# Two attention + FFN layers on one core: VectorE exponentials as four shifted bit patterns summed by PE, one weight ring, LayerNorm transposes by DMA

## The chip, the cores and the metric

The kernel runs on one core of one Trainium2 chip. The metric is device time in microseconds (us) of one execution; where a number is a median, its runs are named. PE is the matrix engine (PEld its weight loads), ACT is ScalarE, DVE is VectorE, POOL is GpSimd, SP issues the DMAs. SBUF and PSUM are the two on-chip memories in which the tiles lie; PE writes its results into PSUM (tile `ps` in the lines below). "The profile" is a page on one execution; "the trace" is what that page is made from. A line number such as L875 is a line of the kernel that the profile is of; an inserted line shifts the numbers below it.

## The reference

Two layers, each an attention block and an FFN, with LayerNorm in front of each and a residual around each:

```python
def _A_ref(x, wqkv, wo):                     # B=1, S=2048, D=512, H=32 heads of 16
    qkv = (x @ wqkv).reshape(B, S, 3, H, 16) ...
    scores = einsum("bhqd,bhkd->bhqk", q, k) * 16 ** -0.5
    p = softmax(scores, axis=-1)
    o = einsum("bhqk,bhkd->bhqd", p, v)
    return o.reshape(B, S, D) @ wo
def _B_ref(x, w1, b1, w2, b2):               # F=1792
    return gelu_tanh(x @ w1 + b1) @ w2 + b2
x = x + _A_ref(layernorm(x)); x = x + _B_ref(layernorm(x))   # twice
```

The scores are the large part: 2 layers x 32 heads x 2048 x 2048. The kernel cuts them into 4096 "cells" of 128 keys x 512 queries of one head.

## The kernel before

A small scheduler in Python builds the instruction order of every engine before the launch. Each piece of work is a generator that yields operations with a guessed cost; the scheduler picks the ready one of the highest priority. On the chip the order is then fixed: an engine whose next instruction waits does nothing else meanwhile.

Per cell, PE makes the scores in a PSUM bank (2 KB a partition), ACT or DVE exponentiates them into SBUF, and PE multiplies the result with V. A V block has 17 columns, the last of them ones, so that the same matmul gives the sum of the exponentials. A pass that takes results out of PSUM, and so frees the bank, is called an eviction here. ACT takes cells in groups of three and two banks; some cells go to DVE, through one of two spare banks (6 and 7), which the projections, the FFN and the transposes need too.

```python
SLOTS = ((0, 1, 2), (3, 4))                       # banks of ACT's two groups
    # exps(): ACT, 2 or 3 cells at a time
    yield _Op("act", ..., lambda e, ...: e.activation(out=dst, in_=src, func=ACT.Exp, scale=0.25), ...)
    # dfirst(): DVE takes a cell out of PSUM as a bf16 bit pattern of 2**x with a linear mantissa
    yield _Op("dve", DV, lambda e: e.tensor_scalar(T["DU"][:, du, j, :], self.bank(b), E_SCALE, E_BIAS,
              op0=ALU.mult, op1=ALU.add), ...)
    # dchain(): three cells at a time, six passes that correct the mantissa
    ... tensor_scalar(m, u, 127, None, op0=ALU.bitwise_and)
    ... tensor_scalar(x, m, -128.0, None, op0=ALU.add)
    ... tensor_tensor(out=x, in0=x, in1=m, op=ALU.mult)
    ... tensor_scalar(v, m, E_B, E_A, op0=ALU.mult, op1=ALU.add)
    ... tensor_tensor(out=v, in0=x, in1=v, op=ALU.mult)
    ... tensor_tensor(out=u, in0=u, in1=v, op=ALU.add)
```

The FFN runs in the background of the attention. Its GELU takes three passes on POOL, a tanh on ACT and one pass on DVE, for 49 pairs of 128-row blocks (the last query chunk uses ACT's own GELU):

```python
    # hpair(): x2 and g2 are 128 x 1024
    yield _Op("pool", 2.2, lambda e: e.tensor_tensor(out=x2, in0=g2, in1=g2, op=ALU.mult), ...)
    yield _Op("pool", 0.8, lambda e: e.tensor_scalar(x2, x2, 8.0 * C2, 2.0 * C1, op0=ALU.mult, op1=ALU.add), ...)
    yield _Op("pool", 2.2, lambda e: e.tensor_tensor(out=x2, in0=x2, in1=g2, op=ALU.mult), ...)
    yield _Op("act", 1.05, lambda e: e.activation(out=x2, in_=x2, func=ACT.Tanh), ...)
    yield _Op("dve", 1.15, lambda e: e.scalar_tensor_tensor(out=g2, in0=x2, scalar=1.0, in1=g2, op0=ALU.add, op1=ALU.mult), ...)
```

The softmax here doesn't subtract the row's maximum and nothing guards it: scores larger than these inputs give would overflow.

Of the kernel before, what the change touches and what calls it, by code (L numbers as in the profile page):

```python
# [12 lines left out]
D = 512  # L13
H = 32
# [5 lines left out]
SLOTS = ((0, 1, 2), (3, 4))  # L20
CELLS = 3
PT_RING = 5
QP_RING = 3
W1_RING = 3

DB = 3
DU = 3
DMIN = 24
LOG2E = 1.4426950408889634
E_SCALE = 0.25 * LOG2E * 128  # L30
E_BIAS = 127.0 * 128
E_A = 0.0023795
E_B = 0.00061147 / 128
# [133 lines left out]
class _Sched:  # L167
# [17 lines left out]

    def spawn(self, gen, prio):
        self.threads.append(_Thread(gen, prio, self.nseq))
        self.nseq += 1

    def _advance(self, th):  # L190
        moved = False
        while th.op is None and not th.done:
# [25 lines left out]
            if isinstance(item, _Op):  # L218
                th.op = item
                if item.prio is None:  # L220
                    item.prio = th.prio
            elif item[0] in ("acq", "need", "take", "cond"):
                th.block = item
            elif item[0] == "rel":
                self.pools[item[1]].append(item[2])
            elif item[0] == "give":
                self.tokens[item[1]] = item[2] if len(item) > 2 else True
            elif item[0] == "spawn":
                self.spawn(item[1], item[2])
# [63 lines left out]
def bass_interleave_layers__mha_block__dense_activation_gelu__prompt_kernel(  # L293
# [15 lines left out]
    with ExitStack() as es:  # L309
        def sb(shape, dt, name):  # L310
# [4 lines left out]
        T["WQKV"] = sb([128, 3, NDC, D], BF16, "wqkv")  # L315
        T["WO"] = sb([128, NDC, D], BF16, "wo")
        T["W1"] = sb([128, W1_RING, NDC, 256], BF16, "w1")
# [8 lines left out]
        T["XN"] = sb([128, NDC, 512], BF16, "xn")  # L326
        T["XLN"] = sb([128, 3, D], BF16, "xln")
        T["G"] = sb([128, NFC, 512], BF16, "g")
        T["X2"] = sb([128, 2, 1024], BF16, "x2")
        T["PT"] = sb([128, PT_RING, CELLS, 512], BF16, "pt")  # L330
        T["PART"] = [v[:, 0:8192].bitcast(F32).rearrange("p (g q) -> p g q", g=8) for v in vf[::-1]]
        T["DU"] = sb([128, DU, DB, 512], U16, "du")
        T["DM"] = sb([128, DB * 512], U16, "dm")
        T["DW"] = sb([128, DB * 512], F16, "dw")
# [17 lines left out]
        sem_names = ["pe", "act", "dve", "pool", "dx0", "dx1", "dx2", "dx3", "dwq", "dwk", "dwv", "dwo", "db1", "db2",  # L352
                     "dw10", "dw11", "dw12", "dw2", "dout"]
# [28 lines left out]
MM = 0.22  # L382
SW = 0.11
ST = 0.36
# [4 lines left out]
class _Plan:  # L389
# [8 lines left out]
    def init(self):  # L398
# [11 lines left out]
        yield _Op("dve", 0.6, lambda e: e.memset(self.bank(5), 0.0), writes=["B.5"])  # L410
# [9 lines left out]
    def loads(self):  # L420
# [22 lines left out]
        yield load(T["WO"][:], hbm["wo"].rearrange("(c p) f -> p c f", p=128), "dwo", ["WO"], 2.5)  # L443
# [32 lines left out]
    def ln_tile(self, c, t, dst, dkeys):  # L476
# [4 lines left out]
            reads=["X.%d" % t, "RSTD.%d" % c, "NMR.%d" % c], writes=["XLN.%d" % x])  # L481
        b = yield ("acq", "misc")
# [10 lines left out]
    def proj(self, l, kind, i, c, src, skeys, ph, done):  # L493

        T = self.T
        for t in ([i] if kind == "V" else range(4 * c, 4 * c + 4)):
            yield ("need", ("lnt", t, ph))
        b = yield ("acq", "misc")
        pb = self.bank(b)
        W = T["WQKV"]  # L500
        w = "QKV".index(kind)
        fns = []
        for dc in range(NDC):
            if kind == "V":
                fns.append(lambda e, dc=dc: e.matmul(pb, lhsT=src(dc, i), rhs=W[:, 2, dc, :], start=(dc == 0),
                                                     stop=(dc == NDC - 1)))
            else:
                fns.append(lambda e, dc=dc: e.matmul(pb, lhsT=W[:, w, dc, 128 * i:128 * (i + 1)], rhs=src(dc, None),  # L508
                                                     start=(dc == 0), stop=(dc == NDC - 1)))
        reads = ["W.%d" % w] + (skeys[i % 4:i % 4 + 1] if kind == "V" else skeys)  # L510
        for h in range(0, 4, 2):
            yield _Op("pe", SW + 2 * MM, fns[h:h + 2], reads=reads, writes=["B.%d" % b])
# [18 lines left out]
    def projections(self, l, c, prio):  # L531
# [5 lines left out]
        else:  # L537
            def src(dc, t):
                return T["XN"][:, dc, (t % 4) * 128:(t % 4) * 128 + 128] if t is not None else T["XN"][:, dc, :]
            skeys = ["XN.%d" % j for j in range(4)]  # L540
        ph = self.phase[c]
        units = []
        for b in range(4):
            units.append(("K", b))
            if l == 1 or c == 0:
                units.append(("Q", b))
            units.append(("V", 4 * c + b))
        if l == 0 and c > 0:
            units += [("Q", b) for b in range(4)]
        for kind, i in units:  # L550
            p = prio + (0.5 if kind == "Q" and c > 0 else 0)
            yield ("spawn", self.proj(l, kind, i, c, src, skeys, ph, (kind, l, i, c)), p)
# [35 lines left out]
    def wo(self, l, c, t):  # L588
        T = self.T
        for gb in range(4):  # L590
            yield ("need", ("otn", l, c, gb))
        b = yield ("acq", "misc")
        pb = self.bank(b)
        q = slice((t % 4) * 128, (t % 4) * 128 + 128)
        fns = [lambda e, j=j: e.matmul(pb, lhsT=T["OTN"][:, j, q], rhs=T["WO"][:, j, :], start=(j == 0), stop=(j == 3))  # L595
               for j in range(4)]
        for h in range(0, 4, 2):
            yield _Op("pe", SW + 2 * MM, fns[h:h + 2], reads=["WO"] + ["OTN.%d" % j for j in range(4)],
                      writes=["B.%d" % b])
# [5 lines left out]
    def w1loads(self):  # L605
        T = self.T
        yield ("need", "loaded")
        for l in range(NL):
            for c in range(self.NQ):
                for p in range(NFC // 2):  # L610
                    w = yield ("acq", "w1")
                    yield _Op("sp", 1.5, lambda e, w=w, p=p: e.dma_start(
                        T["W1"][:, w, :, :], self.hbm["w1"][:, 256 * p:256 * (p + 1)].rearrange("(c p) f -> p c f", p=128)),
                        writes=["W1.%d" % w], sem="dw1%d" % w, by=16, tail=2.5)
                    yield ("give", ("w1", l, c, p), w)

    def hpair(self, l, c, p):
# [5 lines left out]
        w = yield ("need", ("w1", l, c, p))  # L623
        for j in range(2):
# [4 lines left out]
                pb, lhsT=T["W1"][:, w, dc, j * 128:(j + 1) * 128], rhs=T["XF"][:, dc, :], start=(dc == 0),  # L629
                stop=(dc == NDC - 1)) for dc in range(NDC)]  # L630
            for h in range(0, 4, 2):
                yield _Op("pe", SW + 2 * MM, fns[h:h + 2], reads=["W1.%d" % w] + ["XF.%d" % i for i in range(4)],
                          writes=["B.%d" % b])
            if j == 1:
                yield ("rel", "w1", w)
            if last:
# [7 lines left out]
                reads=["B.%d" % b, "HB1T"], writes=[gk[j]])  # L644
            yield ("rel", "misc", b)
        if last:
# [11 lines left out]
        yield _Op("dve", 1.15, lambda e: e.scalar_tensor_tensor(out=g2, in0=x2, scalar=1.0, in1=g2, op0=ALU.add, op1=ALU.mult),  # L658
                  reads=xk + gk, writes=gk)
# [3 lines left out]
    def ytile(self, l, c, t):  # L663
# [9 lines left out]
        for h in range(0, NFC + 1, 2):  # L673
            yield _Op("pe", SW + 2 * MM, fns[h:h + 2],
                      reads=["W2", "ONES1", "B2row"] + ["G.%d" % f for f in range(h, min(h + 2, NFC))],
                      writes=["B.%d" % b])
# [4 lines left out]
        if l == NL - 1:  # L681
            yield _Op("sp", 1.0, lambda e: e.dma_start(self.hbm["out"][:, t, :], T["X"][:, t, :]), reads=["X.%d" % t],
                      writes=["OUT.%d" % t], sem="dout", by=16, tail=2.0)

    def post(self, l, c):
# [6 lines left out]
        for t in tiles:  # L692
            yield ("need", ("xready", t, 2 * l + 1))
        self.phase[c] = 2 * l + 1
        yield ("spawn", self.ln(c, lambda t: T["XF"][:, :, (t % 4) * 128:(t % 4) * 128 + 128],
                                lambda t: ["XF.%d" % (t % 4)], 11), 11)
        for t in tiles:
            yield ("need", ("lnt", t, 2 * l + 1))
        for p in range(NFC // 2):
            yield ("spawn", self.hpair(l, c, p), 12 + 0.1 * p)  # L700
# [4 lines left out]
        if l == NL - 1:  # L705
            return
        self.phase[c] = 2 * l + 2
        yield ("spawn", self.ln(c, lambda t: T["XN"][:, :, (t % 4) * 128:(t % 4) * 128 + 128],
                                lambda t: ["XN.%d" % (t % 4)], 14), 14)
# [26 lines left out]

    def setup_attention(self):
        self.pas = self.passes()
        self.cells = [(pi, kt, a) for pi, p in enumerate(self.pas) for kt in p[3] for a in range(4)]
        self.left = {}  # L740
        for pi, kt, a in self.cells:
            self.left[pi] = self.left.get(pi, 0) + 1
        self.done = {(pi, a): [] for pi in range(len(self.pas)) for a in range(4)}
        self.ptleft, self.duleft = {}, {}
        self.togo = []
        for pi, p in enumerate(self.pas):
            n = 4 * len(p[3])
            self.togo += [n - i for i in range(n)]

    def qpad(self):  # L750
        T = self.T
        for pi, (l, qc, g, kts, part, final) in enumerate(self.pas):
# [3 lines left out]
            yield _Op("pool", 1.5, lambda e, s=s, b=b, t=t, qc=qc: e.tensor_scalar(  # L756
                T["QP"][:, s, :], T["Q"][:, b, 512 * qc:512 * qc + 512], T["MASK"][:, t:t + 1], None, op0=ALU.mult),
# [13 lines left out]

    def scores(self):
        at, u, nd = 0, 0, 0
        pools = self.s.pools
        batch = None
        while at < len(self.cells):
            sl = yield ("acq", "s")
            n = len(SLOTS[sl])
            last = self.cells[min(at + n, len(self.cells) - 1)]
            extra = None  # L780
            room = self.togo[at + n] if at + n < len(self.cells) else 0
            if last[0] == self.cells[at][0] and room >= DMIN and pools["misc"] and (batch or pools["du"]):
                extra = pools["misc"].pop(0)
                if batch is None:
                    batch = (pools["du"].pop(0), [])
                n += 1
            cells = list(self.cells[at:at + n])
            at += len(cells)
            fns, reads, qss, writes = [], [], [], []
            if extra is not None:  # L790
                k = [i for i, c in enumerate(cells) if c[2] == nd % 4]
                dcell = cells.pop(k[0] if k else -1)
                nd += 1
                qs = yield ("need", ("qp", dcell[0]))
                yield ("need", ("K", self.pas[dcell[0]][0], self.pas[dcell[0]][2] // 2, dcell[1] // 4))
                f, r = self.score(dcell, qs, extra)
                dfn = f
                reads += r
                writes.append("B.%d" % extra)
# [178 lines left out]
```

## Time and profile before

| | before |
|---|---|
| median time | 1960.8 us |
| span of the profiled run | 1958.2 us |
| ACT busy | 1783.9 us (91%) |
| PE busy, mean granted clock | 1590.1 us (81%), 0.725 |
| DVE busy | 1228.5 us (63%) |
| POOL busy | 429.4 us (22%) |
| cells on ACT / on DVE | 3759 / 337 |

These are lines of the page of the kernel before: busy time by engine, the granted clock of PE in 40 slices of the span in tenths, and the chain that ended last, by engine.

```profile
PE 1590.1 (81%) x9782; PEld 382.9 (20%) x9889; DVE 1228.5 (63%) x1909; ACT 1783.9 (91%) x1577; POOL 429.4 (22%) x253
...
PEclk9975568885768858778587875877568855689558
...
ACT 60%; PE 18%; DVE 10%; POOL 6%; issue 6%; DMA 0%; POOLq 0%
```

ACT is nearly always busy and makes up most of the chain: it sets the pace. PE is often at half clock (5), above all where attention runs alone.

The groups view of the kernel before: line, engine, operation, output and input, shapes, count, then busy time and mean of one in ns, then the engine's idle time before them.

```profile
L875 ACT ACTIVATE pt<-ps 128x1536 bf16<-128x1536 f32 x1504 | 1724.9, 1299 | 100.7 <-PE ps L769 68.7
...
L833 DVE TENSOR_SCALAR du<-ps 128x512 uint16<-128x512 f32 x337 | 229.1, 683 | 168.0 <-PE ps L769 164.6
```

3759 cells in 1724.9 us make 0.459 us of ACT for a cell. The second line counts the DVE cells.

Finally a stretch of the timeline of the kernel before, where POOL works on GELU: start, duration, engine, line, operation.

```profile
328.49 0.60 DVE L852 TENSOR_SCALAR dm<-du 128x1536 uint16<-128x1536 uint16 x1
328.64 2.44 POOL L656 TENSOR_TENSOR x<-x,g 128x1024 bf16<-128x1024 bf16 x1
329.13 2.36 DVE L853 TENSOR_SCALAR dw<-dm 128x1536 f16<-128x1536 uint16 x1
```

L852 took 0.60 us and started before the POOL pass. L853, a pass of the same width whose median is 0.56 us, started within it and lasted 2.36 us, until after POOL had ended.

### The profile page before, as it was taken

What the parts mean: (1) busy time and instruction counts of PE and PEld (TensorE: products, weight loads), DVE (VectorE), ACT (ScalarE), POOL (GpSimd) and SP (SyncE); (2) the same over time, 40 slices, a digit from 0 to 9 for tenths busy, and PEclk for the clock granted to TensorE, in tenths of its full rate; (3) what the DMA queues carried; (4) which work ended last, traced back from release to release, by engine and by line L of the source; (5) the groups of instructions that cost most, each with busy time, mean ns of one, the idle gap of its engine ahead of it and who ended that gap; (6) DMA issues with size and microseconds to landing.
All of it is one profiled execution on the core that took longest, in us unless ns stands there. A gap on an engine that the chain in (4) does not pass through costs nothing.

```text
span 1958.2 us, 23879 instructions
## 1 busy us (share of the span) xinstructions
PE 1590.1 (81%) x9782; PEld 382.9 (20%) x9889; DVE 1228.5 (63%) x1909; ACT 1783.9 (91%) x1577; POOL 429.4 (22%) x253
## 2 busy tenths in 40 slices
PE   6888887888868888788887888868887788868887
PEld 2221121221212212121121211211112211212113
DVE  6357887357684585746765424575776577773872
ACT  6989999999979999899998999889998999989992
POOL 3101018110260004500045011450007100170000
PEclk9975568885768858778587875877568855689558
DMA  4000001000000000000000000000001000010001
GB/s 140 1 1 1 1 1 38 1 1 1 17 22 1 1 1 22 17 1 1 1 22 17 1 1 1 28 14 9 1 1 38 9 3 1 6 33 12 1 1 33
DMA packets 38042, 24.34 MB, mean 12 GB/s; under 512 B 1325, under 2 KB 37934, under 8 KB 37934
## 3 DMA queue, kind: packets, MB, share of 16 engines
q1 hardware_dynamic: 37934, 22.82, 3.9%
q8 instruction: 78, 1.28, 0.3%
q14 instruction: 30, 0.25, 0.0%
HBM read 20.71 MB, written 2.10 MB: 12 GB/s over the span
## 4 chain that ended last, share of the span: by engine, by line
ACT 60%; PE 18%; DVE 10%; POOL 6%; issue 6%; DMA 0%; POOLq 0%
ACT pt L875 59%; PE ps L769 6%; PE ps L909 4%; POOL x L653 2%; PE ps L628 2%; DVE du L833 2%; POOL x L656 2%; PE ps L670 2%; DVE g L658 2%; POOL x L654 1%; PE ps L484 1%; DVE dw L853 1%; PE ps L595 1%; DVE dw L854 1%; PE ps L508 1%
## 5 line engine op out<-in xcount | busy, mean ns | idle before, releaser
L875 ACT ACTIVATE pt<-ps 128x1536 bf16<-128x1536 f32 x1504 | 1724.9, 1299 | 100.7 <-PE ps L769 68.7
L769 PE MATMUL ps<-qp,kt 32*128 32x512 bf16 x4096 | 762.2, 507 | 284.3 <-ACT pt L875 244.5
L909 PE MATMUL ps<-pt,v 128*17 128x512 bf16 x3759 | 519.5, 499 | 25.1 <-DVE du L857 21.4
L756 POOL TENSOR_SCALAR qp<-q,mask 128x512 bf16<-128x512 bf16 x80 | 129.0, 1613 | 1118.8 <-PE ps L769 1110.8
L769 PEld LDWEIGHTS ps<-qp,kt 32*128 32x128 bf16 x4096 | 156.2, 95 | 951.9 <-ACT pt L875 688.6
L833 DVE TENSOR_SCALAR du<-ps 128x512 uint16<-128x512 f32 x337 | 229.1, 683 | 168.0 <-PE ps L769 164.6
L909 PEld LDWEIGHTS ps<-pt,v 128*17 128x17 bf16 x3759 | 95.9, 89 | 336.7 <-issue 267.0
L628 PE MATMUL ps<-xf,w 128*128 128x512 bf16 x419 | 123.9, 413 | 17.4 <-DVE g L642 11.6
L670 PE MATMUL ps<-w,g 128*128 128x512 bf16 x413 | 124.9, 409 | 7.4 <-issue 5.5
L909 PE MATMUL ps<-du,v 128*17 128x512 bf16 x337 | 124.9, 541 | 1.9 <-DVE du L857 1.8
L677 DVE TENSOR_TENSOR x<-x,ps 128x512 bf16<-128x512 bf16 x32 | 21.9, 684 | 164.1 <-PE ps L672 164.1
L642 DVE TENSOR_SCALAR g<-ps,hb1t 128x512 bf16<-128x512 f32 x98 | 71.9, 746 | 80.7 <-PE ps L628 80.5
L854 DVE TENSOR_TENSOR dw<-dw,dm 128x1536 f16<-128x1536 f16 (+2 forms) x121 | 116.6, 964 | 3.5
L653 POOL TENSOR_TENSOR x<-g 128x1024 bf16<-128x1024 bf16 x49 | 98.2, 2004 | 91.3 <-DVE g L642 66.5
L656 POOL TENSOR_TENSOR x<-x,g 128x1024 bf16<-128x1024 bf16 x49 | 112.5, 2297 | 3.0
L856 DVE TENSOR_TENSOR dm<-dw,dm 128x1536 f16<-128x1536 f16 (+2 forms) x121 | 109.5, 905 | 3.1
L857 DVE TENSOR_TENSOR du<-du,dm 128x1536 uint16<-128x1536 uint16 (+2 forms) x121 | 108.9, 900 | 2.7
L658 DVE SCALAR_TENSOR_TENSOR g<-x,g 128x1024 bf16<-128x1024 bf16 x49 | 78.1, 1594 | 29.1 <-ACT x L657 28.5
L853 DVE TENSOR_SCALAR dw<-dm 128x1536 f16<-128x1536 uint16 (+2 forms) x121 | 79.4, 656 | 2.8
L467 POOL TENSOR_TENSOR rstd<-varr,nhalf 128x4 f32<-128x4 f32 x16 | 19.2, 1199 | 272.8 <-DVE varr L465 272.8
L852 DVE TENSOR_SCALAR dm<-du 128x1536 uint16<-128x1536 uint16 (+2 forms) x121 | 72.2, 597 | 2.2
L855 DVE TENSOR_SCALAR dm<-dm 128x1536 f16<-128x1536 uint16 (+2 forms) x121 | 71.8, 593 | 2.8
(58 smaller groups left out, 818.2 us busy)
## 6 DMA issues: line engine op xcount, KB each, us to landing
w<-in_B_w_dram SPq DMA_DIRECT2D x56, 256.0 KB, 2.8
x<-in_A_x_dram SPq DMA_DIRECT2D x4, 512.0 KB, 8.3
out_dram<-x SPq DMA_DIRECT2D x16, 128.0 KB, 1.7
w<-in_B_w_dram SPq DMA_DIRECT2D x1, 1792.0 KB, 12.0
wqkv<-in_A_wqkv_dram SPq DMA_DIRECT2D x3, 512.0 KB, 5.9
wo<-in_A_wo_dram SPq DMA_DIRECT2D x1, 512.0 KB, 7.1
b1c<-in_B_b_dram SPq DMA_DIRECT2D x1, 3.5 KB
b2row<-in_B_b_dram SPq DMA_DIRECT2D x1, 1.0 KB
```

The costliest lines, as they stand in the source:

```text
L628: fns = [lambda e, dc=dc, j=j, pb=pb: e.matmul(pb, lhsT=T["W1"][:, w, dc, j * 128:(j + 1) * 128], rhs=T["XF"][:, dc, :], start=(dc == 0), ...
L653: yield _Op("pool", 2.2, lambda e: e.tensor_tensor(out=x2, in0=g2, in1=g2, op=ALU.mult), reads=gk, writes=xk)
L656: yield _Op("pool", 2.2, lambda e: e.tensor_tensor(out=x2, in0=x2, in1=g2, op=ALU.mult), reads=gk + xk, writes=xk)
L658: yield _Op("dve", 1.15, lambda e: e.scalar_tensor_tensor(out=g2, in0=x2, scalar=1.0, in1=g2, op0=ALU.add, op1=ALU.mult), reads=xk + gk, w ...
L670: fns = [lambda e, fc=fc: e.matmul(pb, lhsT=T["G"][:, fc, q], rhs=T["W2"][:, fc, :], start=(fc == 0), stop=False) for fc in range(NFC)]
L756: yield _Op("pool", 1.5, lambda e, s=s, b=b, t=t, qc=qc: e.tensor_scalar(T["QP"][:, s, :], T["Q"][:, b, 512 * qc:512 * qc + 512], T["MASK" ...
L769: return (lambda e: e.matmul(o, lhsT=lhsT, rhs=rhs, start=True, stop=True, tile_position=(32 * a, 0)), ["K%d.%d.%d" % (l, g // 2, kt // 4) ...
L833: yield _Op("dve", DV, lambda e: e.tensor_scalar(T["DU"][:, du, j, :], self.bank(b), E_SCALE, E_BIAS, op0=ALU.mult, op1=ALU.add), reads=[" ...
L854: yield _Op("dve", tt, lambda e: e.tensor_tensor(out=x, in0=x, in1=m, op=ALU.mult), reads=["DM", "DW"], writes=["DW"])
L856: yield _Op("dve", tt, lambda e: e.tensor_tensor(out=v, in0=x, in1=v, op=ALU.mult), reads=["DM", "DW"], writes=["DM"])
L875: yield _Op("act", 0.065 + 0.4267 * n, lambda e, src=src, dst=dst: e.activation(out=dst, in_=src, func=ACT.Exp, scale=0.25), reads=["B.%d" ...
L909: fns.append(lambda e, o=o, lhsT=lhsT, rhs=rhs, a=a, st=count[a] == 0, sp=count[a] == n - 1: e.matmul(o, lhsT=lhsT, rhs=rhs, start=st, sto ...
```

## The change

Its intent is to move exponentials from ACT to DVE by making a DVE cell much cheaper. The six correcting passes go. DVE writes the rough pattern of 2**x, then adds constants to the bit pattern to get three copies shifted by a quarter, a half and three quarters of an octave (an octave is a factor of two). PE multiplies the four patterns by V and by three scaled copies of V, all into the same accumulator: the errors of the four linear mantissas largely cancel. PE pays four PV matmuls for such a cell instead of one. Cells of 4 of the 16 key tiles may go this way, at most 1024.

```diff
-    def dchain(self, du, cells):            # the six passes above
+        # dcell(): one cell
+        yield _Op("dve", 0.68, lambda e: e.tensor_scalar(D4[:, 0, :], self.bank(b), E_SCALE, E_BIAS, op0=ALU.mult, op1=ALU.add), ...)
+        yield _Op("dve", 0.20, lambda e: e.tensor_scalar(D4[:, 1, :], D4[:, 0, :], SHIFT, None, op0=ALU.add), ...)
+        if self.turn == 0 and self.s.clock["pool"] < self.s.clock["dve"] + 0.1:     # at most every third cell
+            yield _Op("pool", 1.36, lambda e: e.tensor_scalar(hi, lo, 1.0, 2.0 * SHIFT, op0=ALU.mult, op1=ALU.add), ...)
+        else:
+            yield _Op("dve", 0.34, lambda e: e.tensor_scalar(hi, lo, 2 * SHIFT, None, op0=ALU.add), ...)
+        for i in range(4):                  # four PV matmuls, with V and three scaled copies
+            ...
+    def vcopies(self):                      # POOL scales V, 3 copies for 4 key tiles a layer
```

Around it, buffers are freed and the background work is rearranged:

```diff
-        # T["WQKV"], T["WO"], T["W1"]: resident or with rings of their own
+        T["WR"] = sb([128, W_RING, 1024], BF16, "wr")     # one ring of 5 for Wo, W1 and layer 1's Wqkv
-        # PE transposes of the LayerNorm output, copied out of PSUM by DVE
+            yield _Op("sp", 0.3, lambda e: e.dma_start(dst(t), T["XLN"][:, x, :], transpose=True), ...)   # all but the first chunk
+            yield ("cond", self.when(l, c, 0.06 + (0.06 if l else 0.055) * p))   # FFN spread over the chunk
-        yield _Op("dve", 1.15, lambda e: e.scalar_tensor_tensor(out=g2, in0=x2, scalar=1.0, in1=g2, ...)
+        yield _Op("dve", 0.34, lambda e: e.tensor_scalar(x2, x2, 1.0, None, op0=ALU.add), ...)
+        yield _Op("dve", 0.62, lambda e: e.tensor_tensor(out=g2, in0=x2, in1=g2, op=ALU.mult), ...)
```

Bank 7 is lent to DVE cells unless the other users queue. PV runs in up to two rounds of four matmuls. The three GELU passes on POOL stay, with an fp16 scratch in place of bf16. POOL's masking pass on the queries (80 times) gets a second operation, a multiplication by 1.0.

## The prediction

> **What bounds the kernel now.** ScalarE. The page's busy shares give ACT 1783.9 us of 1958.2 (91%), PE 81%, DVE 63%, POOL 22%. The chain that ended last is 60% the exp activation. The groups view: 3759 of the 4096 score cells (128x512) are exponentiated on ACT in 1724.9 us, 0.459 us a cell; only 337 go to VectorE. PE is second because its clock is low: mean granted clock 0.725, and 0.50 in stretches with attention alone (windows view, 150 to 250, 1350 to 1450 us), where matmul groups start every 0.54 us instead of 0.32.
>
> **What changes.**
> - A VectorE cell now costs 2.34 us of DVE: eviction 0.68 (229.1/337) plus a six-pass polynomial, 1.66 (558/337). After: eviction 0.69, one 512-wide add (0.28, the fastest 512-wide pass) and one 1024-wide add (0.42, interpolated to the 1536-wide 0.56), a third of the latter on POOL. About 1.25 to 1.4 us with the semaphore gaps. So DVE can take over twice as many cells: at most 1024 are eligible (4 of 16 key tiles); bank and buffer limits make me expect about 850 (700 to 1000).
> - ACT: about 3250 cells x 0.459 + 59 us of other work = 1550 us, 235 less.
> - DVE: 440 us of other work now; less 25 (copies of LN transposes) and about 25 (GELU product split into faster passes), plus 850 x 1.3: about 1500 us. It becomes the second bound, 80 to 90% busy.
> - PE: 3 more PV matmuls per such cell, about 2500 more, four side by side: some 640 extra rounds x 0.2135 us = 140 us warm, 270 at half clock.
> - A gain: FFN and projections are spread over each query chunk, and PV streams more, so PE should fall to half clock less often. I expect a mean granted clock of 0.85 or more. The Trainium skill ("TensorE: Matmul & The Clock Gate", Part 1) says activity releases the throttle; this trace agrees: at 262 us the clock rose to 1.0 after about 5 us of nearly gapless matmuls.
> - A loss: the skill ("SBUF — State Buffer", Who interferes with whom) says VectorE's two-port modes and GpSimd lock each other out. This trace agrees: at 329 to 335 us, with POOL busy, 1536-wide DVE passes took 2.36 us instead of 0.56. The new DVE passes are of this kind and POOL gets about 250 extra 1.36 us passes. I allow 60 to 150 us of longer DVE passes.
> - Weight ring and DMA transposes: off the critical path except at the tail after the last exp (50 us now), where the LN transposes by DMA add perhaps 5 us.
>
> **Sum.** The path stays ACT-led, but three engines are nearly balanced in a static order. I expect ACT busy about 1550 us at 88% of the span: 1755 us. Range 1640 to 1870. Chances: faster 0.86, within 2% 0.09, slower 0.05.
>
> **Right or wrong if.** Exp groups cover about 3250 cells; ACT about 1550 us; DVE 1400 to 1600 us; PE clock at least 0.85; PV matmuls about 6600; waits of ACT on PE larger than now (68.7 + 30.0 us); chain with a smaller ACT share and more DVE. DVE adds slower where POOL runs.
>
> **What would make it wrong.** The port lock costing far more, so that DVE bounds the span (1850 or more); PE staying cold in attention-only stretches (no gain); fewer cells taken than 700; or ACT over 93% busy (1660).

## The result, and the profile after

| | before | after |
|---|---|---|
| median time (4 runs each) | 1960.8 us | 1903.2 us |
| span of the profiled run | 1958.2 | 1899.6 |
| ACT busy | 1783.9 | 1653.7 (87%) |
| ACT idle (span less busy) | 174.3 | 245.9 |
| PE busy, clock | 1590.1, 0.725 | 1553.3 (82%), 0.889 |
| DVE busy | 1228.5 | 1342.6 (71%) |
| POOL busy | 429.4 | 540.3 (28%) |
| cells on ACT / on DVE | 3759 / 337 | 3463 / 633 |

The ratio of the times is 0.970, with a 95% interval of 0.968 to 0.973. All ratios here are made from the fast runs of the same rounds, so not quite the ratios of the medians. The change is faster, by 3% where 10% was predicted, and outside the predicted range.

ACT lost 130 us of work, and 72 us came back as idle time of ACT. The same parts of the page as before:

```profile
PE 1553.3 (82%) x11548; PEld 372.8 (20%) x11548; DVE 1342.6 (71%) x2561; ACT 1653.7 (87%) x1458; POOL 540.3 (28%) x450
...
PEclk9997788899989999789988985989888798997998
...
ACT 46%; PE 26%; DVE 24%; issue 2%; DMA 1%; POOL 0%; SPq 0%; POOLq 0%
```

The clock is up as hoped. The chain has moved from ACT (60% to 46%) to DVE (10% to 24%), although DVE is only 71% busy over the span. An average hides where it is the bound. The groups view of the changed kernel:

```profile
L1004 ACT ACTIVATE pt<-ps 128x1536 bf16<-128x1536 f32 x1385 | 1595.8, 1293 | 186.7 <-PE ps L880 137.7
...
L970 DVE TENSOR_SCALAR du<-ps 128x512 uint16<-128x512 f32 x633 | 429.1, 684 | 280.1 <-PE ps L880 273.9
...
L981 DVE TENSOR_SCALAR du<-du 128x1024 uint16<-128x1024 uint16 x460 | 249.7, 546 | 8.3
L973 DVE TENSOR_SCALAR du<-du 128x512 uint16<-128x512 uint16 x633 | 246.0, 397 | 11.7
```

633 DVE cells, fewer than the lower end (700) that the prediction gave. The eviction from PSUM (L970) takes its 684 ns as ever. But the 512-wide add (L973) averages 397 ns, where its median is 293 ns and its longest 2206 ns; the 1024-wide one (L981) averages 546 ns with a median of 427 ns and a longest of 2339 ns. The tails are what matters.

The windows view shows where ACT is idle: four stretches of 50 us with GELU work, with busy time of each engine and, after the counts, the granted clock and the DMA load.

```profile
300.00:350.00 50.00, 35.41 (x225) 7.53 (x223) 44.88 (x64) 32.61 (x29) 26.55 (x16) 0.83 0.10 27
750.00:800.00 50.00, 36.46 (x223) 7.79 (x220) 45.17 (x59) 32.32 (x28) 27.12 (x17) 0.74 0.08 22
1250.00:1300.00 50.00, 36.56 (x244) 7.73 (x243) 48.30 (x73) 36.12 (x32) 26.20 (x17) 0.80 0.07 22
1450.00:1500.00 50.00, 36.60 (x230) 8.03 (x228) 48.75 (x67) 35.40 (x32) 33.30 (x22) 0.77 0.10 29
```

The columns are PE, PEld, DVE, ACT and POOL. ACT works 32 to 36 us of 50 here, PE 35 to 37, DVE 45 to 49. Taken in slices of 10 us, those that hold a GELU tanh (48 of them, the last 60 us of the span left out) have 116 us of ACT's idle time in the changed kernel and 53 us (36 slices) in the one before; the other slices, without the first 30 us, have 72 and 66. So the idle time that came back, 72 us, is nearly all in the GELU stretches.

The timeline of the changed kernel in one of them shows how one turns into the other:

```profile
321.52 1.90 POOL L728 TENSOR_TENSOR x<-g 128x1024 f16<-128x1024 bf16 x1 [2.67 <-DVE g L717]
...
322.07 1.49 DVE L973 TENSOR_SCALAR du<-du 128x512 uint16<-128x512 uint16 x1
...
323.60 1.23 DVE L981 TENSOR_SCALAR du<-du 128x1024 uint16<-128x1024 uint16 x1
324.63 2.17 POOL L731 TENSOR_TENSOR x<-x,g 128x1024 f16<-128x1024 f16 x1
324.75 0.67 DVE L970 TENSOR_SCALAR du<-ps 128x512 uint16<-128x512 f32 x1
325.34 1.74 DVE L733 TENSOR_SCALAR x<-x 128x1024 f16<-128x1024 f16 x1
325.47 0.10 PEld L880 LDWEIGHTS ps<-qp,kt 32*128 32x128 bf16 x3 [2.19 <-DVE du L970]
...
325.91 1.02 ACT L1004 ACTIVATE pt<-ps 128x1024 bf16<-128x1024 f32 x1 [0.77 <-PE ps L880]
```

The add L973 starts inside the POOL pass L728 and ends 0.14 us after it (323.56 against 323.42) instead of after 0.29 us. The next add (L981) does the same with the POOL pass L729. DVE works in order, so the eviction L970 of the next cell starts at 324.75. Until it is done its bank isn't free, so the score group on PE waits 2.19 us for it, and ACT waits 0.77 us for the scores. The eviction itself isn't slowed: it took 0.67 us with a POOL pass (L731) running nearly all the time.

### The profile page after: what moved, and what is told of

Read it like the earlier page. It is cut to its first block, busy times and chain, and to the rows that moved or that the text cites. A ratio compares the mean times of both kernels' runs of the same rounds, so it can differ in the third digit from the quotient of the medians.

```text
span 1899.6 us, 28436 instructions
## 1 busy us (share of the span) xinstructions
PE 1553.3 (82%) x11548; PEld 372.8 (20%) x11548; DVE 1342.6 (71%) x2561; ACT 1653.7 (87%) x1458; POOL 540.3 (28%) x450
## 4 chain that ended last, share of the span: by engine, by line
ACT 46%; PE 26%; DVE 24%; issue 2%; DMA 1%; POOL 0%; SPq 0%; POOLq 0%
ACT pt L1004 46%; PE ps L1058 10%; PE ps L880 8%; DVE du L970 5%; DVE du L973 5%; DVE du L981 4%; PE ps L704 3%; DVE g L717 3%; PE ps L745 3%; DVE x L733 2%; DVE g L734 2%; PE ps L549 1%; DMA xf<-xln 1%; DVE ott L629 1%; DVE xt L620 1%
## 5 line engine op out<-in xcount | busy, mean ns | idle before, releaser
L1004 ACT ACTIVATE pt<-ps 128x1536 bf16<-128x1536 f32 x1385 | 1595.8, 1293 | 186.7 <-PE ps L880 137.7
L880 PE MATMUL ps<-qp,kt 32*128 32x512 bf16 x4096 | 596.8, 420 | 220.6 <-ACT pt L1004 151.2
L970 DVE TENSOR_SCALAR du<-ps 128x512 uint16<-128x512 f32 x633 | 429.1, 684 | 280.1 <-PE ps L880 273.9
L978 POOL TENSOR_SCALAR du<-du 128x1024 uint16<-128x1024 uint16 x173 | 184.7, 1068 | 824.9 <-DVE du L973 813.0
L1058 PE MATMUL ps<-du,vc 128*17 128x512 bf16 x1899 | 389.5, 431 | 1.6 <-DVE du L973 1.3
L880 PEld LDWEIGHTS ps<-qp,kt 32*128 32x128 bf16 x4096 | 144.1, 92 | 860.2 <-ACT pt L1004 461.9
L981 DVE TENSOR_SCALAR du<-du 128x1024 uint16<-128x1024 uint16 x460 | 249.7, 546 | 8.3
L973 DVE TENSOR_SCALAR du<-du 128x512 uint16<-128x512 uint16 x633 | 246.0, 397 | 11.7
L704 PE MATMUL ps<-xf,wr 128*128 128x512 bf16 x448 | 146.8, 439 | 80.9 <-DVE g L717 59.8
L728 POOL TENSOR_TENSOR x<-g 128x1024 f16<-128x1024 bf16 x49 | 95.3, 1945 | 135.3 <-DVE g L717 127.5
L731 POOL TENSOR_TENSOR x<-x,g 128x1024 f16<-128x1024 f16 x49 | 109.9, 2243 | 3.9
L717 DVE TENSOR_SCALAR g<-ps,hb1t 128x512 bf16<-128x512 f32 x98 | 72.7, 742 | 28.6 <-PE ps L704 28.1
L704 PEld LDWEIGHTS ps<-xf,wr 128*128 128x128 bf16 x448 | 33.0, 103 | 163.9 <-issue 86.2
L729 POOL TENSOR_SCALAR x<-x 128x1024 f16<-128x1024 f16 x49 | 54.5, 1113 | 4.3
```

Of the source, the lines that this page charges most:

```text
L704: fns = [lambda e, dc=dc, j=j, pb=pb: e.matmul(pb, lhsT=T["WR"][:, w, 256 * dc + 128 * j:256 * dc + 128 * j + 128], rhs=T["XF"][:, dc, :], ...
L717: yield _Op("dve", DV, lambda e, fc=fc, pb=pb: e.tensor_scalar(T["G"][:, fc, :], pb, T["HB1T"][:, fc:fc + 1], 0.5, op0=ALU.add, op1=ALU.mult),
L880: return (lambda e: e.matmul(o, lhsT=lhsT, rhs=rhs, start=True, stop=True, tile_position=(32 * a, 0)), ["K%d.%d.%d" % (l, g // 2, kt // 4) ...
L970: yield _Op("dve", 0.68, lambda e: e.tensor_scalar(D4[:, 0, :], self.bank(b), E_SCALE, E_BIAS, op0=ALU.mult, op1=ALU.add), reads=["B.%d" % ...
L973: yield _Op("dve", 0.20, lambda e: e.tensor_scalar(D4[:, 1, :], D4[:, 0, :], SHIFT, None, op0=ALU.add), reads=key[:1], writes=key[1:2])
L978: yield _Op("pool", 1.36, lambda e: e.tensor_scalar(hi, lo, 1.0, 2.0 * SHIFT, op0=ALU.mult, op1=ALU.add), reads=key[:2], writes=key[2:])
```

## The experiments

Theories after this reading. **Lock:** while POOL runs a GELU pass, DVE passes such as the adds stand still (the effect that the prediction calls a loss), evictions come late, PE's score groups wait and ACT starves. **PE:** the added PV rounds delay the score groups. **DVE load:** DVE simply has too much work in those stretches. **Chain:** it is the latency of the GELU chain that holds up the FFN. And apart from them **count:** fewer cells went to DVE than expected.

In e1, e2, e3 and e8 the costs that the order is built with are left as they are and only the emitted instruction is made narrow. Every engine then gets the same order, and only a duration differs. In the other experiments the order is built anew, so that it differs a little beyond the edit named.

### e1: short GELU passes on POOL

```diff
-  e.tensor_tensor(out=x2, in0=g2, in1=g2, op=ALU.mult)      # and the two that follow, 1024 columns
+  e.tensor_tensor(out=xs, in0=gs, in1=gs, op=ALU.mult)      # 64 columns; same modelled cost, same order
+  memset of x2 to zero once at the start
```

> The changed kernel, same order of every instruction on PE, ACT, DVE; the three GELU passes on POOL cut from 1024 to 64 columns (wrong result on purpose). Lock theory (POOL passes hold the port that VectorE's two-port passes need; late evictions starve ScalarE): about 1835 us (1815 to 1855), the 512-wide VectorE add back to a mean of 0.28 to 0.31 us from 0.397, ScalarE idle in the GELU stretches halved. Rival, PE theory (the added PV rounds delay the score groups): 1890 to 1905, little change. It does not tell the lock from the shorter GELU chain.

Measured: 1768.5 us, ratio to before 0.900: 135 us less than the changed kernel, far more than expected. (It passed the comparison with the reference although 15 of 16 columns skip the GELU polynomial, presumably because the tolerance is too wide to see it. It is an experiment, not a kernel to use. That holds for e6, e7 and e8 too.) DVE busy fell from 1342.6 to 1199.5 us, by 143 us, though DVE executes the very same instructions (engine line of the page, then the groups view, of e1):

```profile
PE 1491.6 (84%) x11413; PEld 371.9 (21%) x11548; DVE 1199.5 (68%) x2561; ACT 1643.4 (93%) x1458; POOL 331.5 (19%) x451
...
L983 DVE TENSOR_SCALAR du<-du 128x1024 uint16<-128x1024 uint16 x460 | 210.9, 462 | 8.3
L975 DVE TENSOR_SCALAR du<-du 128x512 uint16<-128x512 uint16 x633 | 185.6, 301 | 11.7
```

The adds are back near their medians: they make up 99 us of the 143, and GELU's own two passes on DVE 40 us. ACT is 93% busy, and its idle time in slices with GELU fell from 116 us to 6 us. The PE theory expected no change, so it falls here.

### e2: short adds on DVE

```diff
-  e.tensor_scalar(D4[:, 1, :], D4[:, 0, :], SHIFT, None, op0=ALU.add)          # and the 1024-wide one
+  e.tensor_scalar(D4[:, 1, 0:16], D4[:, 0, 0:16], SHIFT, None, op0=ALU.add)    # 16 columns each
```

> The changed kernel, same order; VectorE's two add passes of a cell cut to 16 columns (wrong result on purpose). If VectorE's time is what costs, own work plus lock: 1830 to 1860 us, VectorE busy below 1000. PE theory: 1890 to 1905, no change.

Measured: 1863.8 us (wrong result), 39 us less. DVE busy is 1160.4 us, not below 1000. The 16-column adds still averaged 285 and 267 ns. The source view (shortest, median and longest in ns) shows the 512-wide add of the changed kernel, then its 16-column form in e2:

```profile
L973 DVE TENSOR_SCALAR du<-du x633: 221/293/2206, 102.1 to 1841.3; 128x512 uint16<-128x512 uint16 x159
```

```profile
L974 DVE TENSOR_SCALAR du<-du x633: 106/172/2083, 105.3 to 1802.3; 128x16 uint16<-128x16 uint16 x159
```

An add of 16 columns was held up for as long as the full one, up to 2.1 us. And though DVE lost 182 us of busy time here, more than in e1, the span lost only 39. So even taking away nearly all of the adds' width gains less than taking away POOL's passes: width isn't the main cost. GELU's own two passes on DVE were still there, and blocked.

### e3: short PV matmuls for the scaled copies

```diff
+  if begun[a] and self.pvleft[k] > 0 and keys[0].startswith("VC"):
+      o, rhs = o[:, 0:64], rhs[:, 0:64]                     # 64 of 512 columns
```

> The changed kernel, same order; the PV matmuls with the three scaled V copies cut from 512 to 64 columns (wrong result on purpose). PE theory: 1800 to 1850 us. Lock theory: 1885 to 1905, with more idle on PE and possibly a lower granted clock.

Measured: 1914.4 us (wrong result), 11 us more, above both ranges. The PE theory's gain didn't come. The granted clock fell to 0.811 from 0.889: with less to stream, PE spent more time at the low clock, so the extra matmuls pay for part of themselves (PE busy hardly changed, 1550.4 against 1553.3 us). As the clock fell with the work, this run doesn't price the PV matmuls at one clock; against the PE theory stands e1, which left them alone and gained 135 us.

### e4: no share of the adds for POOL

```diff
-  if self.turn == 0 and self.s.clock["pool"] < self.s.clock["dve"] + 0.1:
+  if False:
```

> The changed kernel with the third of the 1024-wide adds that POOL did (173 passes) moved to VectorE; correct result. Lock theory: VectorE gets 173 x 0.43 = 74 us of work but waits less outside the GELU stretches; the two nearly cancel: 1890 to 1915. If the POOL share of the adds were the main source of blocking: 1860 to 1885. If plain VectorE load is what bounds: 1920 or more.

Measured: 1920.7 us, 17 us more, just above the range that the lock theory gave and just inside that of plain DVE load; its runs scatter by 12 us, so it doesn't decide between the two (e5 does). POOL's share of the adds is not the main source of the blocking, and it helps a little.

### e5: the GELU passes on DVE

```diff
-  yield _Op("pool", 2.2, lambda e: e.tensor_tensor(out=x2, in0=g2, in1=g2, op=ALU.mult), ...)
-  yield _Op("pool", 0.8, lambda e: e.tensor_scalar(x2, x2, 8.0 * C2, 2.0 * C1, ...), ...)
-  yield _Op("pool", 2.2, lambda e: e.tensor_tensor(out=x2, in0=x2, in1=g2, op=ALU.mult), ...)
+  yield _Op("dve", 0.68, ...)   # the same three passes
+  yield _Op("dve", 0.46, ...)
+  yield _Op("dve", 0.68, ...)
```

> The changed kernel with the three polynomial passes of GELU on VectorE in place of POOL (correct result): about 49 x (0.69 + 0.43 + 0.69) = 89 us more work for VectorE, but no POOL pass of 2 us that shuts it out. Lock theory: 1780 to 1840 us. If VectorE is simply overloaded: 1900 or more.

Measured: 1777.4 us, just below the range expected, ratio 0.906 (0.904 to 0.908), with the full GELU. This beats both kernels. DVE was given three more passes for each of 49 pairs and its busy time fell, from 1342.6 to 1241.3 us. (In the order built anew POOL also took 202 of the 1024-wide adds, not 173, and DVE 626 cells, not 633; so DVE had 36 fewer wide adds, 424 for 460, and 7 fewer evictions and narrow adds: by the medians some 20 of the 101 us, an estimate.) The engine line of the page, then stretches of 50 us with GELU work, in the same view as above (PE, PEld, DVE, ACT, POOL):

```profile
PE 1500.1 (84%) x11390; PEld 371.7 (21%) x11527; DVE 1241.3 (70%) x2658; ACT 1648.7 (93%) x1461; POOL 325.0 (18%) x332
...
300.00:350.00 50.00, 42.99 (x346) 10.74 (x344) 48.08 (x105) 49.40 (x46) 10.58 (x8) 0.97 0.11 33
500.00:550.00 50.00, 43.05 (x339) 11.15 (x341) 48.33 (x100) 49.90 (x46) 9.25 (x8) 1.00 0.13 38
```

DVE is as busy here (48 of 50 us) as in the changed kernel (45 to 49), and from 300 to 350 us does 105 instructions in 50 us where that one did 64. ACT is busy throughout. This is where the DVE load theory falls: a full DVE does no harm here, a blocked one does. In the waits view, score groups of PE (L880) waiting for the eviction of a DVE cell (L970), and FFN matmuls (L704) for DVE's pass that takes the FFN's hidden values out of PSUM (L717), first of the changed kernel, then of e5 (us in total, times, longest; PE and PEld wait at the same time, so their totals don't add up):

```profile
PEld ps L880 <- DVE du L970: 97.2, 89, 5.2
PE ps L704 <- DVE g L717: 59.8, 38, 4.8
PE ps L880 <- DVE du L970: 41.2, 38, 4.9
```

```profile
PEld ps L880 <- DVE du L970: 36.3, 44, 1.2
PE ps L704 <- DVE g L717: 6.0, 13, 1.2
```

The long waits are gone: 5.2 us was the longest, now 1.2. The late evictions of the FFN were a part of them beside those of the cells.

### e6: POOL load outside the GELU chain

```diff
   # the passes of e1, here with modelled costs of 0.3 each, and after the product that ends the chain, on the same scratch:
+  pool: tensor_tensor(out=x2, in0=x2, in1=x2, op=ALU.mult)
+  pool: tensor_scalar(x2, x2, 0.0, 0.0, op0=ALU.mult, op1=ALU.add)
+  pool: tensor_tensor(out=x2, in0=x2, in1=x2, op=ALU.mult)
```

> As e1 (short GELU passes), plus three full-width POOL passes per pair after the GELU chain is done, on the same scratch, for which nothing waits in time. POOL load of the changed kernel, chain as short as in e1; 64 of 1024 columns get the polynomial. Lock theory: back up to 1860 to 1910. Chain theory (the GELU chain's latency holds up the FFN): 1760 to 1785.

Measured: 1877.9 us. Passes that nothing waits for cost 109 us, and the adds are slow again (groups view of e6):

```profile
L986 DVE TENSOR_SCALAR du<-du 128x1024 uint16<-128x1024 uint16 x451 | 251.9, 563 | 8.1
L978 DVE TENSOR_SCALAR du<-du 128x512 uint16<-128x512 uint16 x627 | 237.0, 385 | 11.9
```

That is the lock without the chain. It gives back 109 of e1's 135 us, and DVE's busy time is up by 110 us again (1309.5 against 1199.5). The passes stand at another place and the order has 627 cells instead of 633; which of these makes up the other 26 us isn't settled.

### e7: a long GELU chain without POOL

```diff
   # the passes of e1, here with modelled costs of 0.3 each, and between the last one and the tanh:
+  sp: dma_start(sc, xs)        # 16 KB to a second scratch
+  sp: dma_start(xs, sc)        # and back
```

> As e1, plus two DMA hops of some 2 us in each GELU chain: chain as long as in the changed kernel or longer, POOL nearly idle. Lock theory: 1760 to 1800. Chain theory: 1860 to 1910.

Measured: 1767.6 us, the same as e1, with 633 cells as there. The hops took 1.7 us each (median, issue to landing) and the three short passes 0.9 us together, so the chain lasted about 4.3 us before the tanh; the changed kernel's passes sum to 5.3 us and e1's to 1.0. The latency that e1 had removed was mostly put back and cost nothing. The chain theory falls.

### e8: short GELU passes in the kernel before

The same edit as e1, in the kernel before.

> The kernel before, same order, with the three GELU passes on POOL cut to 64 columns. If the lock costs the kernel before as much as the changed one (135 us by e1): about 1825. If the change made the kernel sensitive to it, because before VectorE was off the critical path: 1900 to 1940, a gain of 20 to 60 us.

Measured: 1902.4 us, ratio 0.970, within the second range, with a gain of 60 us at its edge. So the lock was there before too, but the same POOL work costs 135 us after the change. DVE's busy time fell by 61 us (1228.5 to 1167.2), again as much as the time: what the change raised is how much of DVE's time POOL blocks, not what a blocked microsecond costs.

### e9: fewer DVE cells

```diff
   # e5
-DU = 5
+DU = 3
```

> e5 with three instead of five buffers for VectorE cells: 450 cells in place of 626 by the order built. If ScalarE's cell count sets the pace once the lock is gone, 176 x 0.459 = 81 us more: 1840 to 1870 us. If PE or VectorE sets it: 1780 to 1800.

Measured: 1871.0 us, just above the range expected, with 450 DVE cells against e5's 626: 93 us for 176 cells, 0.53 us a cell. ACT busy went from 1648.7 to 1732.4 us, by 84 us. Once the lock is out, ACT's count of cells sets the pace, and each cell moved is worth what it costs ACT or a little more.

### e10: no spread of the background work

```diff
   # e5
-  return lambda: self.scored >= min(self.base[(l, c)] + part * self.span[(l, c)], self.total)
+  return lambda: True
```

> e5 with the FFN and projection work no longer held back to be spread over the query chunk. If the spread keeps the PE clock up and matters: clock 0.85 or lower and 1800 to 1840 us. If the added PV rounds alone keep the clock up: clock about 0.90 and 1775 to 1795.

Measured: 1791.0 us, 14 us more than e5, at the same clock (0.909 in both profiled runs). The spread gains a little, but not through the clock.

### e11: LN transposes on PE

```diff
   # e5
-  if self.phase[c] or c:       # DMA transpose
+  if False:                    # PE transposes and DVE copies
```

> e5 with all LN transposes back on PE (with their PSUM copies on VectorE). If the DMA transposes are worth what they save on PE and VectorE (some 25 us of VectorE): 1785 to 1800. If their 2.4 us of latency costs as much in the tail and at the layer switch: 1765 to 1780.

Measured: 1779.7 us, against 1777.4. No difference beyond the scatter of the runs. Whatever the DMA transposes save on DVE (1241.3 against 1267.2 us busy) is not on the path here.

### e12: the kernel before with GELU on DVE

e5's edit in the kernel before.

> The kernel before with the three GELU passes on VectorE. By e8 the lock cost it some 60 us and VectorE had 37% to spare: 1900 to 1925. If the polynomial passes of its cells leave VectorE no room: 1950 or more. Beside e5 this gives the change's worth with the lock taken out of both.

Measured: 1914.8 us, ratio 0.975. With the lock taken out of both, the change is worth 1914.8 - 1777.4 = 137 us, or 7%; the pair e8 and e1 gives nearly the same, 1902.4 - 1768.5 = 134 us. With it, 58 us. ("Taken out" is meant of the GELU passes; POOL's other passes still run.)

## Why the prediction was wrong

The prediction was 1755 us, range 1640 to 1870; measured 1903.2.

**The bound and the mechanism (right).** ACT set the pace before, and with the lock out of the way moving cells helps at about the rate predicted: 0.459 us a cell by the profile, 0.53 by e9, and 137 us for 291 cells, 0.47 each, between e12 (335 cells) and e5 (626). With the lock in place it did not: 58 us for 296 cells, 0.19 each.

**The number of cells (wrong).** "Bank and buffer limits make me expect about 850 (700 to 1000)": there are 633. So "about 3250 cells" on ACT are 3463, and "1550 us" of ACT are 1653.7: 104 us of the 148 us missed. The limit named was the right one, but its size was guessed. Counted while the order is built (in Python, not on the chip), of 1385 score groups 262 were filled up with DVE cells, 790 found no free PSUM bank and 465 no free buffer (some neither); in only 62 were both free with no cell to take. e9 shows on the chip what a smaller buffer ring does to the count and to the time.

**The lock (seen, but in no term of the sum).** The prediction had read the 2.36 us passes out of the trace and allowed "60 to 150 us of longer DVE passes". The inflation was indeed 143 us (e1). But no term holds it: DVE's "about 1500 us" is already 440 - 50 + 850 x 1.3, and "ACT busy about 1550 us at 88% of the span" leaves ACT 205 us of idle time for everything, against 174 before; measured 246 us with the lock, 122 us without (e1: a span of 1765.9 less 1643.4). It was thought of as busy time of DVE, "the second bound", where it belonged on the path of ACT. Blocked DVE time went into the time almost one for one: 143 us of DVE and 135 us of time in e1, 110 and 109 between e1 and e6, 61 and 60 in e8. DVE's own work did not: e2 took 182 us off DVE and 39 us off the time. The step that failed is the one that took DVE's share of the whole span for its weight: in the stretches where POOL works, DVE was the bound, and its blocked passes stand in front of the evictions that free PE's banks.

So two steps failed, the number of cells and the place of the lock. Without GELU's part of the lock the time is inside the range even with 633 cells: e1 measured 1768.5 us. What the missing cells cost under the lock no run shows: 217 more would be worth 100 us at 0.459 us each (an estimate), but a cell moved under the lock brought less. Two errors of size partly cancel in the sum: ACT's work was put too low by 104 us, and its idle time apart from the lock too high by about 83 us (205 - 122).

**PE's clock and load (right in size, half right in cause).** The clock is 0.889, at least 0.85 as said. About half of the rise from 0.725 is the streaming of the added PV matmuls (e3: 0.811 with most of it cut); the spread has no share in it (e10: no difference), and what makes up the other half wasn't tested. The trace of the kernel before doesn't show what releases the clock: it rose at 262 us after 5 us with PE busy for 4.6, but from 161 to 166 us PE was busy for 4.91 us and the clock stayed at 0.50 for another 96 us. "PV matmuls about 6600": 3463 + 4 x 633 = 5995, as the cells were fewer.

**Waits and chain (right, but for DVE's busy time).** ACT waits on PE are 137.7 + 44.2 us, larger than 68.7 + 30.0; ACT's share of the chain is smaller and DVE's larger. DVE busy 1342.6 us (71%) is below the 1400 to 1600 (80 to 90%) said.

**Weight ring and DMA transposes off the path (right as far as tried).** e11 shows no effect of the transposes. The ring was not undone, since the SBUF that it frees is used; its cost stays untested, beyond the DMA load of 22 GB/s.

**"What would make it wrong".** It listed "the port lock costing far more, so that DVE bounds the span (1850 or more)" and "fewer cells taken than 700". Both came, the first only in the GELU stretches.

What stays open: the remaining 26 us between e6 and the changed kernel, and half of the rise of the clock.

## What to carry to other kernels

When a change gives an engine many short passes of a kind that another engine can shut out, look for the stretches where both run, and count the blocked time there in full on the span, not as busy time of an engine with an idle average. Test it by making the other engine's instructions narrow while keeping the order: that took one run here, and the repair, moving the slow engine's three passes onto the "loaded" engine, made that engine less busy and the kernel 126 us faster. And when a new path depends on free banks and buffers, count how many pieces the order will really take before multiplying by the gain of each.

## What the Trainium skill lacked or had wrong

- "SBUF — State Buffer", section Who interferes with whom, says that a DVE two-port pass and a GpSimd instruction shut each other out for a whole instruction, and that a DVE instruction with at most one SBUF input outside those modes isn't affected. The runs agree: the 512-wide add took up to 2.2 us against a median of 0.29, the PSUM eviction never over 0.69. What it lacks is the size of the consequence in a whole kernel: cutting 260 us of POOL's GELU passes to 49 us gave back 143 us of DVE time and 135 us of the time (e1), and 61 and 60 us in the kernel before (e8).
- Its summary (section Summary: rules for kernel authors) says of running both engines at once: "Schedule whichever is off the critical path". Here it was better not to run both: giving POOL's GELU passes to DVE saved 126 us (e5), although DVE was already 90 to 98% busy in the four stretches shown of the changed kernel.
- "TensorE: Matmul & The Clock Gate", Part 1, says that a busy window of about 3.4 us brings the full clock and an idle one takes it away, but not how busy is busy. In the kernel before PE was at 0.50 from 150 to 250 us, at 84% and 83% busy in the profile (two halves), even through 5 us with 98% (161 to 166 us). In the changed kernel the same window had 0.76 and 0.80 at 82% and 79% busy, with more matmuls (609 against 496). The profile's busy share of PE doesn't tell which clock follows. And PV matmuls with V blocks of only 17 columns bear on the clock: most of the added ones cut short, it was 0.811 against 0.889 (e3).
- No page has this: GpSimd's tensor_scalar of 128x512 bf16 took 1613 ns on average with one operation (kernel before) and 731 ns with a second, a multiplication by 1.0, added (changed kernel).
